# A global-filter and maxout kernel: the step plan of batches 1 to 5 rearranged

## The chip, the core and the metric

The kernel runs on one core of a Trainium2 chip. The metric is the device time of one execution in microseconds. A core has a matrix engine (TensorE, PE in the profile, with its weight loads on a line of their own, PEld), a vector engine (VectorE, DVE), a scalar engine (ScalarE, ACT), a general engine (GpSimd, POOL) and a sync engine (SyncE, SP) that here only starts transfers. Each engine takes its instructions in the order in which the program lists them, and waits at one until what it needs is there. Transfers (DMAs) are started by SP or by POOL and run on 16 DMA engines.

## What is computed

Two stages, one after the other. First each of 8 batches of a sequence (3072 positions, 256 channels) is filtered along the sequence in the frequency domain; then each position goes through a maxout layer.

```python
X = np.fft.rfft(x, axis=1)                       # x: 8 x 3072 x 256
Y = X * (filt_r + 1j * filt_i)[None, :, :]
y = np.fft.irfft(Y, n=x.shape[1], axis=1)
...
g = np.maximum(y @ w1, y @ w2)                   # hidden width 1024
out = g @ w_out                                  # 24576 x 256
```

## The kernel before, in words

The transform of length 3072 is split into 128 by 24, so that each part is a set of small matrix products. One batch passes through these stations:

- **x load** (`load_p`, line 393): six loads c = 0 to 5 for a batch, each of two DMAs of 256 KB, issued by SP into the tile `xf`.
- **fold** (`fold_x`, line 402): POOL adds and subtracts the two halves of `xf` and writes the bf16 tile `xd`; two instructions for each load.
- **S1** (`f1_half`, lines 404 to 414): PE multiplies `xd` into `pa`, ACT copies `pa` to `at` and SP writes `at` to the scratch memory `ad`.
- **bt read** (`f1_read`, lines 416 to 423): eight DMAs on SP read `ad` back in another order, into the tile `bt`. The rows of 256 bf16 values that it moves are 512 bytes long.
- **S2 and S3** (`gen_f2`, lines 432 to 483): PE multiplies `bt` into `px` (line 469), VectorE multiplies by the filter into `pq` (474), PE multiplies `pq` into `pz` (447), ACT copies that to `zt` (451), and SP writes `zt` to the scratch memory `zd` (456).
- **z read** (`z_read`, line 429): two DMAs on SP, one for each half of the partitions, read `zd` into `zr`; each waits until the writes that it needs have landed.
- **s4** (lines 574 to 586): PE multiplies `zr` into `py`, ACT and VectorE scale it into the tile `yt`, which feeds the second stage.

The second stage is cut into 48 tiles of 512 positions, six for each batch. One tile takes 8 **steps**. A step has one `moe_h` (line 610: two matmuls into `ph`, then a relu into `gt` by ACT, or by VectorE where line 612 says so) and one `moe_o` of the tile before (lines 630 and 635, into `po`). At the eighth step of a tile POOL starts the output's DMA (line 642, 512 KB from `ot`, of which there are two buffers). The maxout is computed as max(h1 - h2, 0) with h2's part added by the matrix `M`.

The second stage of one batch hides the first stage of the next ones. The loop at the end of the kernel (lines 795 to 806) runs over steps 0 to 391, emits `moe_h` and `moe_o` of the step, and then what the table `todo` holds for it; `plan(step, fn, ...)` fills the table by hand. `plan_x` puts the six loads of a batch at given steps and each fold 12 steps behind its load. `plan_f2` puts nine calls of the generator `gen_f2` at given steps, and the two z reads. A call emits S2 of one group of eight and S3 of the group before; the ninth call has only the last S3. In six of the nine calls S1 of the *next* batch (`f1_half`) goes first. `spaced(first, gap, count)` gives the steps; `in_f2` (line 793) lists the stretches of steps in which VectorE takes no relu.

A step is a place in the order of the program, not a time: PE, ACT and VectorE follow the steps closely, since they have work in each. SP has none of its own and runs ahead down its list until an item has to wait. The first s4 of a batch comes at its predecessor's sixth tile: for batch 1 at step 47, for batch 2 at 94, for batch 3 at 142 (line 805).

Of the kernel before, what the change touches and what calls it, by code (L numbers as in the profile page):

```python
# [29 lines left out]
def kernel(  # L30
# [573 lines left out]
    def moe_h(tt, j):  # L604
        if j == 0:
            gt[tt] = gpool.tile([128, 8, 512], BF16, tag="gt", name="gt")
        y_ = yt[tt]
        ph = ps.tile([128, 512], FP32, tag="ps")
        for dc in range(2):
            TE.matmul(ph, Wd[:, dc, 128 * j:128 * j + 128],  # L610
                      y_[:, dc].rearrange("p a b -> p (a b)"), start=(dc == 0), stop=(dc == 1))
        if j in (1, 5) and not in_f2(8 * tt + j):
            V.tensor_scalar(gt[tt][:, j], ph, 0.0, None, OP.max)  # L613
        else:
            S.activation(gt[tt][:, j], ph, AF.Relu)  # L615
# [125 lines left out]
    def plan(step, fn, *a):  # L741
        todo.setdefault(step, []).append((fn, a))

    def plan_x(n, steps, lag=12):
        for c, s_ in enumerate(steps):
            plan(s_, load_p, n, c)
            plan(s_ + lag, fold_x, n, c)

    def plan_f2(n, steps, z1, z0):
        g = []  # L750

        def go():
            if not g:
                g.append(gen_f2(n))
            next(g[0], None)

        for s_ in steps:
            plan(s_, go)
        plan(z1, z_read, n, 1)
        plan(z0, z_read, n, 0)  # L760

    def spaced(first, gap, count):
        return [first + int(gap * i) for i in range(count)]
# [3 lines left out]
    for c in range(4, 12):  # L767
        plan(int(0.6 * (c - 3)), f1, 1, c, (S, V)[c % 2])
    plan(5, f1_read, 1)
    plan_f2(1, spaced(15, 2.4, 9), 28, 36)  # L770
    for c in range(3):
        plan(6 + c, load_p, 2, c)
        plan(7 + 2 * c, fold_x, 2, 3 + c)
        plan(15 + 2 * c, fold_x, 2, c)
    plan(36, f1_read, 2)
    plan_x(3, spaced(24, 3, 6))
    plan_f2(2, spaced(60, 2.5, 9), 74, 81)
    plan(83, f1_read, 3)
    plan_x(4, spaced(64, 3.5, 6))
    plan_f2(3, spaced(104, 3, 9), 121, 129)  # L780
    plan(130, f1_read, 4)
    plan_x(5, spaced(108, 3.5, 6))
    plan_f2(4, spaced(150, 3.3, 9), 168, 178)
    plan(179, f1_read, 5)
    for n in range(5, B):
# [4 lines left out]
        plan_f2(n, spaced(197 + o, 3.4, 9), 216 + o, 226 + o)  # L790

    def in_f2(step):
        return 0 <= step < 6 or 15 <= step < 36 or 60 <= step < 82 or 104 <= step < 130

    for tt in range(6 * B + 1):
        b, i = divmod(tt, 6)
        for j in range(8):
            step = 8 * tt + j
# [38 lines left out]
```

## Time and profile before

| What | Value |
|---|---|
| Median of 8 runs | 528.24 us (527.36 to 530.29) |
| The profiled execution | 527.82 us |
| Its span, first to last instruction | 526.0 us |
| Mean granted clock of PE | 0.997 of full speed |
| First call of S2/S3 of batch 1, step 15, reached by PE | 65.03 us |
| Call at step 17 | 70.32 us |
| First s4 of batch 1, step 47, begins | 112.87 us |
| First call of batch 2, step 60 | 128.85 us |
| First call of batch 3, step 104 | 184.08 us |
| First call of batch 4, step 150 | 241.19 us |
| z reads of batch 1 issued | 90.40 and 106.53 us |
| x loads, all batches | 72 issues of 256 KB on SP |
| DMA traffic of the whole execution | 97.03 MB, 184 GB/s on the mean |

How to read the profile: for each group of instructions it gives the line of the kernel, the engine, the operation and the tiles (out<-in), the number of instructions, and busy times. A wait is named by the engine and line that stood still, an arrow, and the engine or transfer that released it. In a timeline the first number is the start in microseconds from the beginning of the span, the second the length; idle time of the engine just before stands in brackets. A queue's own line (SPq) shows when a transfer was issued, not when its data had landed. Idle time of an engine costs nothing by itself, unless PE waits behind it in the end.

### The profile page before, as it was taken

Reading aid. Unit: us, or ns where it says so; the run is one execution under the profiler, and the core shown is the slowest. Engines: PE = TensorE matmul, PEld = TensorE weight load, DVE = VectorE, ACT = ScalarE, POOL = GpSimd, SP = SyncE. Lnnn points to the kernel's source line nnn. Section 1 sums busy time; section 2 is a strip of 40 time slices with the busy share of each in tenths; the row PEclk is TensorE's granted clock in tenths of the full one; section 3 lists DMA queues with packets and bytes.
Section 4 is the critical chain, followed back from the end, with each engine's and each line's share of the span. In section 5 each row is a group of like instructions: output and inputs, shape, how many; then the busy total and the mean of one; then the engine's idle time right before and its main releaser. Section 6 shows DMA issues by size and latency. Waiting matters only on the chain.

```text
span 526.0 us, 12529 instructions
## 1 busy us (share of the span) xinstructions
PE 504.4 (96%) x5204; PEld 346.6 (66%) x5282; DVE 322.7 (61%) x438; ACT 336.4 (64%) x598; POOL 148.5 (28%) x168
## 2 busy tenths in 40 slices
PE   8989989979999999999999999999999999999997
PEld 3556656646667666676666666676667766677775
DVE  8987568424783476546883588547773588544442
ACT  6787669625885588846775577646775566545442
POOL 6683524344028203540066002820000000000000
PEclk9999999989999999999999999999999999999999
DMA  7994898997788979897798959994467935341212
GB/s 143 282 199 101 198 228 244 306 179 158 242 222 240 204 199 297 255 183 186 204 246 212 210 157 250 279 197 144 141 172 157 175 111 142 105 126 41 82 60 101
DMA packets 74093, 97.03 MB, mean 184 GB/s; under 512 B 5106, under 2 KB 49780, under 8 KB 73044
## 3 DMA queue, kind: packets, MB, share of 16 engines
q1 hardware_dynamic: 63012, 63.72, 52.7%
q0 software_dynamic: 11024, 32.51, 20.1%
q8 instruction: 41, 0.67, 0.6%
q14 instruction: 16, 0.13, 0.1%
HBM read 54.79 MB, written 47.19 MB: 194 GB/s over the span
## 4 chain that ended last, share of the span: by engine, by line
PE 82%; DMA 10%; ACT 4%; issue 1%; DVE 1%; SPq 0%; POOL 0%; ACTq 0%; POOLq 0%; DVEq 0%
PE po L635 30%; PE ph L610 27%; PE po L630 7%; PE pz L447 4%; DMA zd<-zt 4%; PE py L580 3%; PE px L469 3%; DMA zr<-zd 2%; PE pa L410 2%; DMA Fs<-in_filt_r_dram 1%; DMA bt<-ad 1%; ACT F L514 1%; ACT At L514 1%; DMA ad<-at 1%; PE pz L548 1%
## 5 line engine op out<-in xcount | busy, mean ns | idle before, releaser
L615 ACT ACTIVATE gt<-ph 128x512 bf16<-128x512 f32 x308 | 181.9, 602 | 127.5 <-PE ph L610 126.3
L635 PE MATMUL po<-Wo,gt 128*128 128x256 bf16 x1536 | 230.5, 273 | 3.1
L635 PEld LDWEIGHTS <-gt 128*128 128x128 bf16 x1536 | 150.6, 98 | 58.2 <-issue 0.6
L474 DVE TENSOR_TENSOR pq<-px,F 120x1024 bf16<-120x1024 f32 x112 | 131.8, 1218 | 30.3 <-PE px L469 30.0
L637 DVE COPY ot<-po 128x512 f32<-128x512 f32 x96 | 66.2, 690 | 104.7 <-PE po L635 104.4
L642 POOL DMA_DIRECT2D out_dram<-ot x47 | 25.8, 548 | 322.2 <-DVE ot L637 297.9
L402 POOL TENSOR_TENSOR xd<-xf 128x512 bf16<-128x512 f32 x72 | 89.1, 1269 | 38.1 <-DMA xf<-in_x_dram 29.8
L610 PEld LDWEIGHTS <-Wd 128*128 128x128 bf16 x768 | 70.9, 98 | 21.5 <-issue 13.0
L451 ACT ACTIVATE zt<-pz 112x512 bf16<-112x512 f32 x112 | 60.9, 601 | 17.8 <-PE pz L447 17.2
L613 DVE TENSOR_SCALAR gt<-ph 128x512 bf16<-128x512 f32 x76 | 52.1, 686 | 30.9 <-PE ph L610 25.0
L413 ACT ACTIVATE at<-pa 128x512 bf16<-128x512 f32 x72 | 39.1, 594 | 15.1 <-PE pa L410 13.7
L580 PE MATMUL py<-G,zr 128*128 128x128 bf16 x376 | 29.2, 219 | 3.5 <-DMA zr<-zd 3.1
L580 PEld LDWEIGHTS <-zr 128*128 128x128 bf16 x376 | 24.7, 98 | 6.6 <-issue 5.5
L447 PE MATMUL pz<-pq,VP 56*64 56x256 bf16 x448 | 28.7, 271 | 0.0
L447 PE MATMUL pz<-pq,VQ 56*64 56x256 bf16 x448 | 28.1, 268 | 0.0
L469 PE MATMUL px<-bt,U 48*64 48x256 bf16 x448 | 22.8, 274 | 2.4 <-DMA bt<-ad 2.4
L469 PEld LDWEIGHTS <-U 48*64 48x64 bf16 x448 | 11.5, 106 | 10.5 <-issue 5.5
L530 DVE TENSOR_TENSOR pq<-px,F 120x1024 bf16<-120x1024 f32 x11 | 13.2, 1221 | 3.5 <-ACT F L514 1.9
L447 PEld LDWEIGHTS <-VP 56*64 56x64 bf16 x448 | 13.6, 105 | 2.0 <-issue 1.9
L410 PE MATMUL pa<-xd,C 64*64 64x512 bf16 x144 | 14.8, 400 | 0.0
L514 ACT ACTIVATE F<-pf 128x1024 bf16<-128x1024 f32 x10 | 10.1, 1030 | 6.9 <-PE pf L134 6.9
L447 PEld LDWEIGHTS <-VQ 56*64 56x64 bf16 x448 | 13.4, 106 | 0.0
(389 smaller groups left out, 593.3 us busy)
## 6 DMA issues: line engine op xcount, KB each, us to landing
out_dram<-ot POOLq DMA_DIRECT2D x47, 512.0 KB, 5.3
xf<-in_x_dram SPq DMA_DIRECT2D x72, 256.0 KB
ad<-at SPq DMA_DIRECT2D x42, 256.0 KB
bt<-ad SPq DMA_DIRECT2D x56, 192.0 KB
zd<-zt SPq DMA_DIRECT2D x56, 192.0 KB
zr<-zd SPq DMA_DIRECT2D x14, 768.0 KB
xb<-in_x_dram POOLq DMA_DIRECT2D x12, 256.0 KB, 11.0
wf<-in_moe_w_dram POOLq DMA_DIRECT2D x2, 1024.0 KB, 10.1
```

The source lines that it names most:

```text
L402: G.tensor_tensor(xb[b, c][:, i], xf[:, 0], xf[:, 1], op)
L413: S.activation(at[:, 2 * m:2 * m + 2], pa[m], AF.Copy)
L447: TE.matmul(pz[c][64 * k:64 * k + 64, i], W[64 * c:64 * c + 56, 2 * g + i, k], pq[k][64 * c:64 * c + 56, ri, i], start=(ri == 0), stop=(ri ...
L451: S.activation(zt[0:ROWS, c, o:o + 2], pz[c][0:ROWS], AF.Copy)
L469: TE.matmul(px[k][64 * c:64 * c + 64, i], U[64 * k:64 * k + 48, 4 * g + 2 * i + c], bt_[64 * k:64 * k + 48, t_], start=True, stop=True)
L474: V.tensor_tensor(pq[k][0:FROWS], px[k][0:FROWS].rearrange("p (o i) d -> p o i d", o=1).to_broadcast([FROWS, 2, 2, D]), F[0:FROWS, :, k, 2 ...
L580: TE.matmul(py[:, n], zr[b][:, 4 * i + n, 128 * dc:128 * dc + 128], G1, start=True, stop=True)
L610: TE.matmul(ph, Wd[:, dc, 128 * j:128 * j + 128], y_[:, dc].rearrange("p a b -> p (a b)"), start=(dc == 0), stop=(dc == 1))
L613: V.tensor_scalar(gt[tt][:, j], ph, 0.0, None, OP.max)
L615: S.activation(gt[tt][:, j], ph, AF.Relu)
L635: TE.matmul(p_, g_[:, jj, 128 * n:128 * n + 128], Wo[:, jj], start=False, stop=(jj == 7))
L637: V.tensor_copy(ot[tt][:, n - 1:n + 1], po[tt])
```

## The change

Only the plan and the list in `in_f2` are changed; no instruction is added or taken away.

```diff
-    plan_f2(1, spaced(15, 2.4, 9), 28, 36)
+    plan_f2(1, spaced(17, 2.25, 9), 28, 36)
...
-    plan(36, f1_read, 2)
-    plan_x(3, spaced(24, 3, 6))
-    plan_f2(2, spaced(60, 2.5, 9), 74, 81)
-    plan(83, f1_read, 3)
-    plan_x(4, spaced(64, 3.5, 6))
+    plan(37, f1_read, 2)
+    plan_x(3, spaced(38, 3, 6))
+    plan_f2(2, spaced(58, 2.4, 9), 70, 78)
+    plan(80, f1_read, 3)
+    plan_x(4, spaced(83, 3, 6))
     plan_f2(3, spaced(104, 3, 9), 121, 129)
     plan(130, f1_read, 4)
-    plan_x(5, spaced(108, 3.5, 6))
+    plan_x(5, spaced(132, 3, 6))
     plan_f2(4, spaced(150, 3.3, 9), 168, 178)
...
-        return 0 <= step < 6 or 15 <= step < 36 or 60 <= step < 82 or 104 <= step < 130
+        return 0 <= step < 6 or 17 <= step < 36 or 58 <= step < 79 or 104 <= step < 130
```

In steps, this is:

| What | Before | After |
|---|---|---|
| Batch 1: calls of S2/S3 | 15 17 19 22 24 27 29 31 34 | 17 19 21 23 26 28 30 32 35 |
| Batch 1: z reads | 28, 36 | 28, 36 |
| Batch 2: bt read | 36 | 37 |
| Batch 3: x loads | 24 27 30 33 36 39 | 38 41 44 47 50 53 |
| Batch 3: folds | 36 39 42 45 48 51 | 50 53 56 59 62 65 |
| Batch 2: calls (with S1 of batch 3) | 60 62 65 67 70 72 75 77 80 | 58 60 62 65 67 70 72 74 77 |
| Batch 2: z reads | 74, 81 | 70, 78 |
| Batch 3: bt read | 83 | 80 |
| Batch 4: x loads | 64 67 71 74 78 81 | 83 86 89 92 95 98 |
| Batch 4: folds | 76 79 83 86 90 93 | 95 98 101 104 107 110 |
| Batch 5: x loads | 108 111 115 118 122 125 | 132 135 138 141 144 147 |
| Batch 5: folds | 120 123 127 130 134 137 | 144 147 150 153 156 159 |

The calls of batches 3 (from step 104, with S1 of batch 4) and 4 (from step 150, with S1 of batch 5) keep their steps. S1 comes in the first, second, fourth, fifth, seventh and eighth call, for loads 0 to 5 in this order (in batch 1's calls: in the third to the eighth, for loads 3, 4, 5, 0, 1, 2).

## The prediction

> **What bounds the kernel now.** I read the page's busy times first, then what TensorE (PE) waited for, then its timeline there, then the queues behind those waits.
>
> ```profile
> PE 504.4 (96%) x5204; PEld 346.6 (66%) x5282; DVE 322.7 (61%) x438; ACT 336.4 (64%) x598; POOL 148.5 (28%) x168
> ```
>
> PE is busy for 504.4 of 526.0 us. The change removes no work, so it can only fill or open gaps on PE. After the start-up PE has two gaps that count, both in the first batch's stretch (PE's waits from 60 to 120 us: total, times, longest):
>
> ```profile
> PE py L580 <- DMA zr<-zd: 2.9, 1, 2.9
> PE px L469 <- DMA bt<-ad: 2.4, 2, 1.3
> PE ph L610 <- ACT y__2172 L583: 0.5, 1, 0.5
> ```
>
> PE's timeline (start, us, line, operation, count, idle before in brackets):
>
> ```profile
> 65.03 0.29 PE L469 MATMUL px<-bt,U 48*64 48x256 bf16 x1
> 66.63 0.30 PE L469 MATMUL px<-bt,U 48*64 48x256 bf16 x4 [1.31 <-DMA bt<-ad]
> 68.03 0.30 PE L469 MATMUL px<-bt,U 48*64 48x256 bf16 x3 [1.10 <-DMA bt<-ad]
> ...
> 70.32 0.41 PE L469 MATMUL px<-bt,U 48*64 48x256 bf16 x8
> ...
> 112.87 0.61 PE L580 MATMUL py<-G,zr 128*128 128x128 bf16 x8 [2.89 <-DMA zr<-zd]
> 113.94 1.01 PE L610 MATMUL ph<-y__2172,Wd 128*128 128x512 bf16 x2 [0.46 <-ACT y__2172 L583]
> ```
>
> The px at 65.03 is the call at step 15: bt isn't there yet, and the last piece lands at 68.03. The py at 112.87 is s4 of the first tile of batch 1, at step 47. After that wait, ph takes 1.01 us where it took 0.59: half clock (columns of the stretches: length, busy of PE, PEld, DVE, ACT, POOL, clock, DMA share, GB/s):
>
> ```profile
> 115.00:116.00 1.00, 1.00 (x6) 0.70 (x5) 0.00 (x0) 0.60 (x1) 0.00 (x0) 0.50 1.26 152
> ```
>
> A bare step (ph, then po) is 0.977 us: 0.43 + 0.54 from starts such as 107.87, 108.30 and 108.84, and 11 steps with one s4 take the 11.2 from 98.62 to 109.83. An s4 adds 0.45. SyncE's (SP's) queue shows why zr is late, and how the bt read behind it spreads:
>
> ```profile
> 92.64 2.16 SPq L395 DMA_DIRECT2D xf<-in_x_dram  x2
> 94.89 0.61 SPq L414 DMA_DIRECT2D ad<-at  x1
> 95.55 3.75 SPq L395 DMA_DIRECT2D xf<-in_x_dram  x2
> 99.40 1.49 SPq L456 DMA_DIRECT2D zd<-zt  x2
> 106.53 0.48 SPq L429 DMA_DIRECT2D zr<-zd  x1
> 107.11 7.69 SPq L423 DMA_DIRECT2D bt<-ad  x8
> 114.85 3.62 SPq L395 DMA_DIRECT2D xf<-in_x_dram  x4
> ```
>
> zt was ready at 97.85, but its write waits behind x loads until 99.40, then lands at 106.5. And those x loads behind the bt reads are slow to arrive, as POOL shows:
>
> ```profile
> 125.97 4.95 POOL L402 TENSOR_TENSOR xd<-xf 128x512 bf16<-128x512 f32 x4 [14.30 <-DMA xf<-in_x_dram]
> ```
>
> Issued from 114.85, in at 125.97: 19.4 us after the zr read was issued. In batch 4, where no x load follows the reads, the DMA engines still work for 17 us on zr (issued 224.09), bt and two output tiles:
>
> ```profile
> 229.00:234.00 5.00, 4.95 (x42) 3.69 (x42) 2.08 (x3) 2.92 (x5) 0.81 (x1) 1.00 1.27 160
> ...
> 240.00:242.00 2.00, 2.00 (x24) 1.08 (x23) 0.77 (x3) 0.95 (x2) 0.00 (x0) 1.00 0.64 227
> ```
>
> **What the Trainium skill says.** "TensorE: Matmul & The Clock Gate", section "What's actually happening": an idle window of about 3.4 us halves PE's clock, and it comes back after about as long a busy one. The trace agrees for 2.89 + 0.46 us of idle (clock 0.50 from 114 to 117); 1.31 + 1.10 us at 65 left it at 1.00. "DMA: Bandwidth & Descriptors", section "Queues, rings and completion order": on each DMA engine descriptors are consumed in ring order, and engines go round robin between queues. So an x load that SP issues behind eight bt reads moves after them, while POOL's output writes squeeze in; 19.4 us agrees. Same page, "Why small descriptors are slow": fixed cost per piece. bt is read in 512-byte rows: 160 GB/s at share 1.27 from 229 to 234, against 381 to 412 at 74 to 76 us where x loads move.
>
> **The change part by part.** The sum is made against the profiled execution (527.82 us: span 526.0 and 1.8 around it), which is 0.42 below the median 528.24.
>
> 1. First call from step 15 to 17. Old loss: 65.03 to 70.32 is 5.29 us for a px (0.24) and two steps (1.95): 3.1 lost. New: step 17's px is reached at 65.03 + 1.95 = 66.98. Five of eight matmuls find their pieces (66.63); the rest waits until 68.03, end 68.3 instead of 67.2: 1.1 lost. The reads themselves are untouched. Gain 2.0 (0 if they slip with other traffic, 3.1 if they come early).
>
> 2. zr of batch 1. The last call goes from 34 to 35. Its S3 began at 96.0 in the old run; step 35 ended at 97.65, without that S3 (0.57) and with the gain of 2.0 this is 95.1. Zt is ready 1.76 later as before: 96.9. SP is free, since no x load stands ahead. Zd write to zr issue where no x load is near: 3.95 (396.92 to 400.87), 4.0, 4.6, 5.4 (278.78 to 284.17); I take 4.5: zr issued at 101.4, landed 6.2 later (106.53 to 112.74): 107.6. PE reaches step 47 at 109.98 - 2.0 = 108.0. So no wait, or 0.7 at 5.4. Old loss there: 109.98 to 117.56 is 7.58 for 2.41 of work, 5.17; the 0.46 for y stays. Gain 4.7 (4.0 to 4.7). Batch 2's zr wait of 0.2 goes too. The calls pressed from 2.4 to 2.25 steps cost nothing by what is seen: 22 to 24 and 29 to 31 already run two steps apart, at 3.15 us each, with ACT at 9.3 of 10 us (80 to 90); bound 0 to 0.5.
>
> Gains: 2.0 + 4.7 + 0.2 = 6.9.
>
> 3. x loads of batch 3 from step 24 to 38. Each moved load is two SP issues (0.6 us each[...]) and two POOL folds, 36 of each for three batches; none of it runs on PE, so a move costs only what PE then waits for. SP doesn't wait for steps but runs its list down: zr, eight bt reads (7.7 us of issue), twelve xf issues. The first xf thus lands some time after zr's issue. Above: 19.4 (batch 3's fifth load, old). Below: bt issue to first xf in was 14.5 at batch 2's start (60.60 to 75.13), plus 0.6 between zr and bt issue and 3 for zr's own data (DMA busy 225 to 229 before the slow phase; 1 at 62): 18.1. I take 18.7: 101.4 + 18.7 = 120.1. The fold is two POOL instructions of 1.27 with its start: 122.7. Step 58 needs it (f1_half comes first in the call): 108.0 + 0.45 + 0.46 + 11 x 0.977 + 0.45 = 120.1. So PE stops for 2.6 (1.9 to 3.3), with px, ph and po behind it. Whether the clock drops is open: 0 below, 1.8 above (5.17 - 0.46 - 2.89); I take 0.9. POOL holds output tile 5 behind two folds, until some 125; its buffer is next written at step 67 (135), and outputs beside bt reads took 9.3 us: just in time.
>
> 4. Batch 4: last call at 77, first f1_half at 104. From the last call's start, zr is issued at 6.3 (217.8 to 224.09 in the old batch 3), xf 18.7 later, fold 2.6: 27.6. PE: 0.5 + 27 x 0.977 + three s4 and a y gap (1.8): 28.7. No wait, by 1.1 (0.3 to 1.8).
>
> 5. Batch 5: last call at 128, f1_half at 150, neither moved. zr issued at 224.09 (old clock), xf in at 242.8, fold done 245.4. PE was there at 241.19. It stops for 4.2 (3.5 to 4.9), longer than the idle that halved the clock: 1.8 more. 6.0.
>
> Losses: 3.5 + 6.0 = 9.5. The cover that goes is the steps between a load's place and its first use: 36 in batch 3 before (24 to 60), now 20 (38 to 58); 40 in batch 4, now 21; 42 in batch 5 (108 to 150), now 18. Of these, the SP queue in front takes 9 to 10. The three POOL-to-SP waits of the next loads (batch 6 from step 155 waits for the folds of 150) only reach SP. Relus of step 81 moving to VectorE: nothing, it is 61% busy.
>
> Net 9.5 - 6.9 = +2.6: 530.4 for such an execution, 530.8 at the median.
>
> **Rivals.** (a) The loads come in time: faster. The mechanism is the gap from zr's issue to the first xf. PE doesn't stop in batch 3 if it is under 16.1 us (120.1 - 2.6 - 101.4), in batch 5 under 14.5. For it: bandwidth of 350 and more is seen for x loads, and pieces are spread over 16 engines. Against: 17 us of DMA work without any x load in batch 4. Then 528.2 - 6.9 = 521.3. (b) Shorter stops: batch 3 none, batch 5 3.5 with 1.8 for the clock: 528.2 - 6.9 + 5.3 = 526.6, or 528.0 with 1.4 in batch 3 too. For it: the loads have the queue to themselves once bt is in; against: both measured ends of the gap are above 18. (c) The zr wait stays as well, since zd lands late, with both stops, or POOL's late output tiles hold ot: 528.2 - 2.2 + 9.5 = 535.5. (d) The plan does nothing: excluded, as SP's order is the program's.
>
> **How the numbers follow.** Both stops, 0.50 (own range 529 to 534); (b) 0.17; (a) 0.22; (c) 0.11. 0.3% is 1.6 us, about what can be told from no change. Faster: (a) and 0.05 of (b), 0.27. Same: the rest of (b) and 0.08 of the first, 0.20. Slower: 0.53. The range 522 to 536 leaves out the fast half of (a) and the top of (c).
>
> **What would show it.** zr of batch 1 issued near 101 us and no PE wait at step 47 with clock 1.00; px at step 17 waiting about 1 us; PE waits at the pa matmuls (L410) on POOL's folds at steps 58 and 150, none at 104; POOL's folds of batches 3 and 5 ended by xf. It is wrong if pa waits for nothing there, or if zr is still late.

## The result and the profile after

The changed kernel takes 533.41 us at the median (531.18 to 536.35, 11 runs), the kernel before 528.29 us in the runs beside it (525.69 to 531.13, 32 runs): ratio 1.0093, 95% interval 1.0075 to 1.0111. The profiled execution took 532.27 us with a span of 530.5. It is slower, and most of the loss lies at one place.

PE's waits in the whole of the changed kernel (total, times, longest) have lost the wait for zr, and have a new first line:

```profile
PE pa L410 <- POOL xd L402: 6.8, 4, 4.2
...
PE px L469 <- DMA bt<-ad: 0.6, 1, 0.6
```

The two old gaps, in PE's timeline: px at step 17 waits 0.56 us instead of 2.41, and the s4 of step 47 starts with no wait, 4.73 us earlier than before (112.87):

```profile
66.93 0.40 PE L469 MATMUL px<-bt,U 48*64 48x256 bf16 x5
67.89 0.30 PE L469 MATMUL px<-bt,U 48*64 48x256 bf16 x3 [0.56 <-DMA bt<-ad]
...
108.14 0.61 PE L580 MATMUL py<-G,zr 128*128 128x128 bf16 x8
109.21 0.85 PE L610 MATMUL ph<-y__2154,Wd 128*128 128x512 bf16 x2 [0.46 <-ACT y__2154 L583]
```

The new gaps, in the same timeline: S1 of batch 3 at step 58 stands for two short waits, S1 of batch 5 at step 150 for a long one, and behind that ph takes 1.03 to 1.06 us instead of 0.59. In the kernel before, S1 at step 150 had no wait:

```profile
241.19 0.41 PE L410 MATMUL pa<-xd,C 64*64 64x512 bf16 x4
```

After:

```profile
121.72 0.37 PE L410 MATMUL pa<-xd,C 64*64 64x512 bf16 x1 [0.89 <-POOL xd L402]
122.94 0.41 PE L410 MATMUL pa<-xd,C 64*64 64x512 bf16 x3 [0.85 <-POOL xd L402]
...
241.78 0.39 PE L410 MATMUL pa<-xd,C 64*64 64x512 bf16 x1 [4.24 <-POOL xd L402]
243.00 0.64 PE L410 MATMUL pa<-xd,C 64*64 64x512 bf16 x3 [0.83 <-POOL xd L402]
243.01 1.05 PE L469 MATMUL px<-bt,U 48*64 48x256 bf16 x8
244.00 1.03 PE L610 MATMUL ph<-y__4031,Wd 128*128 128x512 bf16 x2
```

Each stop comes in two parts, since a fold is two POOL instructions: the first pa matmul needs the sum only, the second the difference, 1.2 us later, and the last two come behind it.

Before, SP had sent the last of batch 5's loads ahead of the last z read of batch 3:

```profile
215.57 1.28 SPq L395 DMA_DIRECT2D xf<-in_x_dram  x2
224.09 0.48 SPq L429 DMA_DIRECT2D zr<-zd  x1
```

After, SP's queue shows the order that makes the fold late, here in batches 3 and 5: z read, eight bt reads, then all twelve x loads in one go. POOL starts the fold when the first load is in:

```profile
101.50 0.47 SPq L429 DMA_DIRECT2D zr<-zd  x1
102.09 7.98 SPq L423 DMA_DIRECT2D bt<-ad  x8
110.17 12.89 SPq L395 DMA_DIRECT2D xf<-in_x_dram  x12
...
219.81 0.47 SPq L429 DMA_DIRECT2D zr<-zd  x1
220.39 7.87 SPq L423 DMA_DIRECT2D bt<-ad  x8
228.37 15.47 SPq L395 DMA_DIRECT2D xf<-in_x_dram  x12
```

```profile
120.41 4.93 POOL L402 TENSOR_TENSOR xd<-xf 128x512 bf16<-128x512 f32 x4 [10.55 <-PE ph L610]
...
240.47 2.48 POOL L402 TENSOR_TENSOR xd<-xf 128x512 bf16<-128x512 f32 x2 [8.66 <-DMA xf<-in_x_dram]
```

From the z read's issue to the first load, taken as the start of its fold, it is 18.9 us in batch 3 and 20.7 in batch 5. I call this time the gap. The first of these lines names ph as the releaser of a fold; the naming is an inference of the profile. The transfer that the fold needed began at 110.17, and in a second trace of this kernel the same fold, at 120.55, is put down to the x load.

The start of the same s4 in both kernels' timelines says where the time went:

| s4 at step | before | after | difference |
|---|---|---|---|
| 47 | 112.87 | 108.14 | -4.73 |
| 52 | 120.50 | 114.35 | -6.15 |
| 100 | 179.63 | 175.84 | -3.79 |
| 148 | 238.70 | 234.97 | -3.73 |
| 156 | 249.85 | 254.29 | +4.44 |
| end of the span | 526.0 | 530.5 | +4.5 |

Six microseconds are gained in batch 1, two given back at step 58, eight lost at step 150, and nothing that counts happens after that.

### The profile page after: what moved, and what is told of

The parts are those of the page before. It is cut to its first block, busy times and chain, and to the rows that moved or that the text cites. A ratio compares the mean times of both kernels' runs of the same rounds, so it can differ in the third digit from the quotient of the medians.

```text
span 530.5 us, 12539 instructions
## 1 busy us (share of the span) xinstructions
PE 507.3 (96%) x5204; PEld 348.0 (66%) x5282; DVE 323.2 (61%) x439; ACT 336.2 (63%) x597; POOL 148.2 (28%) x168
## 3 DMA queue, kind: packets, MB, share of 16 engines
q0 software_dynamic: 11024, 32.51, 19.8%
## 4 chain that ended last, share of the span: by engine, by line
PE 79%; DMA 7%; SPq 4%; DVE 4%; ACT 3%; issue 2%; POOL 1%; POOLq 0%; ACTq 0%; DVEq 0%
PE po L635 29%; PE ph L610 26%; PE po L630 7%; PE pz L447 5%; DMA xf<-in_x_dram 4%; SPq L423 3%; PE py L580 3%; PE px L469 3%; PE pa L410 2%; DMA zd<-zt 1%; ACT F L514 1%; DMA bt<-ad 1%; DVE pq L474 1%; POOL xd L402 1%; DMA ad<-at 1%
## 5 line engine op out<-in xcount | busy, mean ns | idle before, releaser
L410 PEld LDWEIGHTS <-C 64*64 64x64 bf16 x144 | 4.5, 103 | 14.9 <-issue 13.4
```

## The experiments

My theory: the gain and the losses are separate terms, set by the order in SP's queue. Rivals are named with each run. All ratios are to the kernel before on the same chip; beside the different runs it took 528.1 to 528.6 us, so changed kernels may be compared to within about half a microsecond.

**One part undone, or one part alone.** First the changed plan with the loads of batch 5 put back:

```diff
-    plan_x(5, spaced(132, 3, 6))
+    plan_x(5, spaced(108, 3.5, 6))
```

> The changed plan with only the x loads of batch 5 put back to steps 108 to 125. Theory: the loss sits at step 150 alone, where PE stood 5.9 us for the late fold and lost 2.5 more at half clock; with it gone 533.4 - 8.4 = 525.0, under the kernel before, and no PE wait on a fold at step 150. Rival (the moved calls and the other loads cost as well, and the stop at step 150 only shows a delay that would surface later): above 529.

Measured: 525.35 us, ratio 0.994 (0.992 to 0.996). That is 8.1 us under the changed kernel. The first pa at step 150 starts without a wait:

```profile
239.53 0.41 PE L410 MATMUL pa<-xd,C 64*64 64x512 bf16 x4
```

So the rest of the change is a gain, and the loads of batch 5 turn it over. The counterpart is the kernel before with this one edit:

```diff
-    plan_x(5, spaced(108, 3.5, 6))
+    plan_x(5, spaced(132, 3, 6))
```

> The kernel before with only the x loads of batch 5 moved to steps 132 to 147. Theory: the stop at step 150 as in the changed kernel, 8 to 9 us: 536.5 to 537.5. Rival (the stop needs the other moves too): under 532.

Measured: 535.37 us, ratio 1.0143 (1.0111 to 1.0175): 6.8 us slower than the 528.56 of the kernel before beside it, about 1 to 2 under what I expected, and beyond the rival. In its trace the stretch from the s4 of step 148 to that of step 156 is 7.7 us longer than before (18.87 against 11.15), with pa waiting 4.79 + 0.64 us. The stop needs none of the other moves. Now the gain. The calls of batch 1 alone:

```diff
-    plan_f2(1, spaced(15, 2.4, 9), 28, 36)
+    plan_f2(1, spaced(17, 2.25, 9), 28, 36)
...
-    ... 15 <= step < 36 ...
+    ... 17 <= step < 36 ...
```

> The kernel before with only the calls of batch 1 moved (from step 17, 2.25 apart). Theory: the gain at step 17 is 2.0 us, but zr still waits behind the x loads of batch 3 and lands near 112.8, so that PE, there 2 us earlier, waits 2 us longer at step 47: 528 to 529, no change. Rival (moving the calls is by itself what freed the zr read): step 47 without a wait, 522.

Measured: 530.18 us, ratio 1.0039 (1.0021 to 1.0057), a little slower rather than level. In SP's queue and at step 47 on PE:

```profile
99.05 1.26 SPq L395 DMA_DIRECT2D xf<-in_x_dram  x2
100.63 0.83 SPq L456 DMA_DIRECT2D zd<-zt  x2
108.26 0.48 SPq L429 DMA_DIRECT2D zr<-zd  x1
```

```profile
114.66 0.59 PE L580 MATMUL py<-G,zr 128*128 128x128 bf16 x4 [6.34 <-DMA zr<-zd]
```

The zd write still stands behind an x load, and takes until 108.2; the wait grows from 2.89 to 6.34 us. The theory had the direction; it had missed that the z read itself would come 1.7 us later. The moved calls don't free zr. The x loads of batch 3 alone do:

```diff
-    plan_x(3, spaced(24, 3, 6))
+    plan_x(3, spaced(38, 3, 6))
```

> The kernel before with only the x loads of batch 3 moved to steps 38 to 53. Theory: the zd write no longer stands behind x loads, zr is issued near 102.3 and landed by 108.6, before PE comes to step 47 at 110; the 5 us of wait and half clock go. First x load in 18.9 us after zr's issue, fold done at 123.8, step 60 reached at 124.0: no stop or under 1 us. 523 to 524. Rival (DMA load, not order, delays zr; the bt read and the x loads behind it are as much load): zr still late, 527 to 529.

Measured: 522.81 us, ratio 0.990 (0.9877 to 0.9923): most of what can be had from the whole change, in one line. SP's queue with no x load ahead of the zd write, and PE at step 60 of that run, where no wait stands before the first fold's user:

```profile
97.59 0.82 SPq L456 DMA_DIRECT2D zd<-zt  x2
101.29 0.47 SPq L429 DMA_DIRECT2D zr<-zd  x1
```

```profile
124.11 0.41 PE L410 MATMUL pa<-xd,C 64*64 64x512 bf16 x4
```

The first fold ran from 121.51 to 124.0, so step 60 is just late enough, where step 58 with PE two microseconds ahead isn't. The mean clock of this execution is 1.000: no gap is left that lowers it.

**What makes the load late: order or amount.** The changed plan, with two of batch 5's loads put ahead of the bt read in SP's queue:

```diff
-    plan_x(5, spaced(132, 3, 6))
+    for c, s_ in enumerate((129, 129, 138, 141, 144, 147)):
+        plan(s_, load_p, 5, c)
+        plan(144 + 3 * c, fold_x, 5, c)
```

> The changed plan with the first two x loads of batch 5 issued at step 129, between the last z read and the bt read, instead of behind the bt read; folds and calls unchanged. Theory (order in SP's queue: a load behind eight bt reads moves after them): the first load is in some 10 us after zr's issue instead of 20.7, no PE wait at step 150, 525. Rival (the sum of the DMA work is the bound): the bt read comes 3 us later and PE waits for it or for a fold at step 150 or 153; 530 or more.

Measured: 526.08 us, ratio 0.9944 (0.9926 to 0.9962). SP's queue and POOL:

```profile
221.72 0.47 SPq L429 DMA_DIRECT2D zr<-zd  x1
222.28 2.60 SPq L395 DMA_DIRECT2D xf<-in_x_dram  x4
224.93 10.18 SPq L423 DMA_DIRECT2D bt<-ad  x8
```

```profile
233.74 4.94 POOL L402 TENSOR_TENSOR xd<-xf 128x512 bf16<-128x512 f32 x4
```

The fold starts at its own place in POOL's list, with no wait, at most 12.0 us after the z read, and at step 150 PE waits neither for it nor for bt. The same transfers in another order, and the stop is gone: it is the order (the amount adds a smaller part, as the next run shows). At 526.08 the run lies a little above the 525 that I gave.

**Why 20.7 us and not 18.7.** The changed kernel without two output DMAs, those of tiles 15 and 16, whose rows stay unwritten:

```diff
-            if tt < 6 * B - 1:
+            if tt in (15, 16):
+                pass
+            elif tt < 6 * B - 1:
```

> The changed kernel without the output DMAs of tiles 15 and 16 (steps 135 and 143), whose rows are left unwritten. Question: why the first x load of batch 5 took 20.7 us from zr's issue and not 18.7. Theory (output tiles squeeze in from POOL's queue, 512 KB each at some 370 GB/s): 2.8 us less, a gap near 18, a stop shorter by as much, perhaps with the clock kept: 527.5 to 530.5. Rival (zr, the bt read and the load fill the time by themselves): gap still over 20, 533.

Measured: 530.59 us, ratio 1.0052 (1.0032 to 1.0073). The z read was issued at 223.31; POOL's fold:

```profile
241.47 2.48 POOL L402 TENSOR_TENSOR xd<-xf 128x512 bf16<-128x512 f32 x2 [23.41 <-DMA xf<-in_x_dram]
```

The gap is 18.2 us, 2.5 less, and 19.9 to 21.1 in the five traces that have both output tiles there. So these tiles account for what went beyond my figure. The stop at step 150 is 1.79 + 0.86 us, and the clock stays at 1.00 from 244 to 252.

**Stop and clock apart.** The changed kernel with matmuls that fill the stop (what they write is overwritten by S1 itself):

```diff
+        if b == 5 and c == 0:
+            for _ in range(20):
+                TE.matmul(pa[0].rearrange("p n d -> p (n d)"), I128, Wd[:, 0, 0:512], start=True, stop=True)
         for m, i in QUADS:
```

> The changed plan with 20 idle-filling matmuls (128x512, 4.3 us) ahead of the first f1_half of batch 5, into the tile that its own matmuls then overwrite. Theory (2.5 us or more of the loss at step 150 are half clock that comes from PE standing idle): the stop stays, the clock stays at 1.00, 530 to 531. Rival (the slow stretch behind the stop comes from something else, as late relus or DMA traffic): 533 to 534.

Measured: 530.54 us, ratio 1.0044 (1.0026 to 1.0062), 2.9 us under the changed kernel. Two stretches of the changed kernel, then about the same place in this run (length; busy PE, PEld, DVE, ACT, POOL; clock, DMA share, GB/s):

```profile
244.00:246.00 2.00, 2.00 (x11) 1.14 (x9) 1.90 (x2) 1.35 (x3) 2.00 (x3) 0.50 1.07 237
246.00:248.00 2.00, 2.00 (x9) 1.10 (x8) 1.05 (x2) 0.60 (x1) 2.00 (x2) 0.50 1.06 236
```

```profile
246.00:248.00 2.00, 1.95 (x15) 1.39 (x15) 2.00 (x3) 1.63 (x4) 2.00 (x3) 1.00 1.06 238
```

The first pa comes 7.36 us behind the s4 of step 148, against 6.81 in the changed kernel, and waits 0.48 + 0.85 us more behind the filling: the lateness is still there, and only the half clock is gone. By the medians about 2.9 of the 8.1 us are clock, by the traces about 2: from the s4 of step 148 to that of step 156 it is 17.23 us here, 19.32 and 19.03 in two traces of the changed kernel. The other way to it is to come later:

```diff
-    plan_f2(4, spaced(150, 3.3, 9), 168, 178)
+    plan_f2(4, spaced(154, 2.8, 9), 168, 178)
```

> The changed plan with the calls of batch 4 begun at step 154 instead of 150 (2.8 apart, so that they end where they ended). Theory with a threshold: PE comes 3.9 us later to the fold, some 1.5 us of stop are left, too short for the clock to drop, so that 6.5 us of 8.4 go: 526.5 to 527.5. Rival (the loss is the lateness of the load alone): 3.9 go, 529.5.

Measured: 527.50 us, ratio 0.9985 (0.9966 to 1.0005): 5.9 us under the changed kernel for 3.9 us of shift. The longest stop of S1 there is 0.56 us at the first fold, less than the 1.5 I gave, with clock 1.00. So more than the shift came back, as it should where the half clock goes with the stop; but this run also sets batch 4's calls closer, which I didn't test by itself.

**The same kernel again**, since the first trace ran at a mean clock of 0.994 and most timed executions at 0.990:

> The changed kernel once more, for a second trace and further times: 533.4 if the first median holds. The first trace had a mean clock of 0.994 where most of the timed executions had 0.990. Theory: the stop at step 58 (1.7 us idle) halves the clock in some executions and not in others, 1 to 2 us; a trace at 0.990 shows half clock at 122 to 126 too. Rival: the clock differs at step 150 only, in the length of the slow stretch.

Measured: 533.07 us, ratio 1.0102 (1.0053 to 1.015), and a trace at 0.990. The stretch behind step 58, first trace and then this one:

```profile
123.00:125.00 2.00, 2.00 (x21) 1.20 (x21) 1.39 (x2) 1.57 (x3) 2.00 (x2) 1.00 1.03 227
```

```profile
123.00:125.00 2.00, 1.92 (x14) 0.79 (x14) 0.82 (x1) 1.08 (x2) 2.00 (x3) 0.52 1.06 239
```

So the stop at step 58 does halve the clock in some executions: here after 1.24 + 0.85 us idle, in the first trace not after 0.89 + 0.85. The first trace is the exception: of the seven traces in all these runs that have this stop, the other six show the half clock behind it. From the s4 of step 52 to that of step 100 it is 63.21 us here and 61.49 in the first trace. This fits the median lying 5.1 us above before and the first trace only 4.5.

**A better plan.** The kernel before with the loads of batch 3 late, batch 1's calls from 17, and batch 2's calls later, not earlier:

```diff
-    plan_f2(1, spaced(15, 2.4, 9), 28, 36)
+    plan_f2(1, spaced(17, 2.25, 9), 28, 36)
...
-    plan(36, f1_read, 2)
-    plan_x(3, spaced(24, 3, 6))
-    plan_f2(2, spaced(60, 2.5, 9), 74, 81)
+    plan(37, f1_read, 2)
+    plan_x(3, spaced(38, 3, 6))
+    plan_f2(2, spaced(62, 2.4, 9), 75, 82)
...
-    ... 15 <= step < 36 or 60 <= step < 82 ...
+    ... 17 <= step < 36 or 62 <= step < 83 ...
```

> The kernel before with the calls of batch 1 from step 17, x loads of batch 3 from step 38, and calls of batch 2 from step 62 (x loads of batches 4 and 5 where they were). Theory: all gains (2.0 at step 17, 5 at step 47) and no stop at step 62, since the fold done near 123 comes before PE: 520.5 to 521.5. Rival (the gain of step 17 is given back at the first fold of batch 3, as in the run with x loads of batch 5 put back): 522.5 to 523.

Measured: 522.25 us, ratio 0.9881 (0.9847 to 0.9915). It beats both kernels, but isn't told apart from the one-line edit at 522.81. Neither figure on record was met: it misses the 520.5 to 521.5 of the theory, and PE waits for no fold, so the rival's reason is not it either. It is 1.6 us ahead of the one-line edit at the s4 of step 52 (114.13 against 115.75) and 0.3 at step 104 (178.70 against 178.97). With calls that end at step 81, zr of batch 2 comes late by 0.88 us; the cause of the other half microsecond is open.

## Why the prediction was right, and where it was off

I predicted 530.8 us (522 to 536), slower by 2.6; it is slower by 5.1. The mechanism held at each of the five places. The size was half of what came: the forecast was a small difference of two larger sums, and the losses were bigger, 10.5 us in the first trace and 12.0 in the second, against gains of 6.2 and 6.4. I had given the direction little more than even odds (0.53).

- **Step 17.** I gave 1.1 us of loss left. From px at 66.93 to the call of step 19 at 70.18 are 3.25 us for 2.2 of work: 1.05. Right.
- **zr of batch 1.** I gave zr's issue at 101.4 and PE at 108.0; measured 101.50 and 108.14. No wait. Together with step 17 the gain is 6.15 at step 52, against my 6.7 without batch 2's 0.2. The cause, x loads ahead of the zd write, is shown by the two runs with one part each: the loads alone bring 5.7 us, the calls alone cost 1.6. (One sum is off a little: with 5.4 us for the zd write the wait would have been 0.5 us, not 0.7.)
- **Batch 3's stop.** I gave a gap of 18.7 from z read to load and 2.6 us of stop, with 0.9 for the clock between 0 and 1.8. Measured in the first trace: a gap of 18.9; the next ph at 123.50 where it would have been at 121.4, so 2.1 us of stop; no drop of the clock. That the gap came out so close is luck: in the eight other traces with these loads it is 19.8 to 20.4. Over the stretch of step 58 the changed kernel loses 2.4 us in the first trace and 4.1 in the second, on both sides of my 3.5.
- **Batch 4.** No stop was right: pa at step 104 starts at 180.29, as the fold begun at 177.80 ends. The margin was all but nothing, not the 1.1 I gave, since the gap was 20.3 us here; in the run with batch 5's loads put back, pa waited 0.37 us at this place.
- **Batch 5's stop** is the term that was mis-sized: 6.0 predicted (4.2 + 1.8), 8.4 measured. Its stop is 5.9: step 150 is reached at 237.54, and ph starts at 244.00 in place of 238.1. The half clock costs 2.5: 244.00 to 249.39 for three steps of 0.977. Two inputs were too small. The gap was 20.7, not 18.7: I read my figure in the kernel before, where one output tile was started within each of the two stretches (at 66.42 and at 111.11), and here there are two, at 223.01 and 231.27; without them it was 18.2. And the clock's price of 1.8 was read where the clock stood at half for 3.4 us (113.96 to 117.37); here it did so for 6.8 (242.00 to 248.83). Filling the stop gave back 2.9.

The rivals: the loads in time (a) didn't happen in the changed kernel, and its point of 14.5 us for batch 5 fits: with the load at most 12.0 us behind the z read the stop was gone, with 18.2 it was not. Shorter stops (b) came about only where I made them, and (c), a zr still late, not at all. That bt's short rows are what makes its read slow was tested by no run.

## What to carry to other kernels

A queue that runs ahead of the compute engines turns a plan of steps into an order: when moving a load, ask what stands in front of it in its own queue, and how long that takes to drain, not how many steps lie between it and its use. A load put behind a slow read to clear the way for one transfer delays the next stage's first input; with two loads ahead of the slow read (526.08 us), or with only the loads moved that were in the way, those of batch 3 (522.81), the gain stays and the loss at step 150 doesn't come. And a stop of PE is priced as the wait plus the slow clock behind it, so that cutting a long stop to under 1 us can be worth more than the microseconds cut: 5.9 us came back for a shift of 3.9.

## What the runs showed that I had not expected

The clock drops after shorter idle times than I took from the 2.89 us of the kernel before. In batch 3's stop, 0.89 + 0.85 us left it at 1.00, while first waits of 1.24, 1.25, 1.31, 1.37, 1.67 and 2.10 us, each with a second one of 0.85 or 0.86, halved it. But 1.79 + 0.86 at step 150 without the two output tiles didn't, nor did 1.31 + 1.10 at step 15 of the kernel before, while 1.06 + 0.66 at the same step did in the run with batch 5's loads alone. No single threshold of idle time fits.

The slow stretches themselves are regular. After the start-up, ten of the twelve traces have them, twelve in all, and each lasts 3.41 or 6.83 us to within 0.01. Two traces have two of them: they begin 119.47 us apart in the second trace of the changed kernel and 174.08 in the run with batch 5's loads alone, which is 35 and 51 times 3.413. This speaks for a clock that changes on a fixed grid. A drop then costs PE some 1.7 us (half of 3.41) for each step of the grid that it lasts and has work in: one in the kernel before, where I read 1.8 us, two at step 150. The Trainium skill, "TensorE: Matmul & The Clock Gate", section "What's actually happening", has a window of about 3.4 us that runs free of the program, and the grid agrees with it. But its full idle window is longer than any of the idle times above. How much of a window must be idle stays open; the measurement decides, and stops of 2 us are not safe.

Behind the bt reads SP needs about 1.1 to 1.3 us for one x load's DMA (12.89 and 15.47 us for twelve), twice the 0.6 that it can take elsewhere (1.27 for two at 251.38). It costs nothing here: S1's first write of batch 5 went out at 244.78, as ACT's copy for it ended at 244.76.
